# Fused attention and two MoE layers: order of SyncE's register reads, the late slot tables, and the queue of the row stores

## The chip, the cores and the metric

The kernel runs on one core of a Trainium2 chip. The metric is the device time of one execution in microseconds (us). TensorE (PE) does the matrix products, VectorE (DVE) and ScalarE (ACT) move and split what leaves PSUM, GpSimd (POOL) does some of the splitting and all gathers, and SyncE (SP) issues almost all other transfers. Each engine runs its own instructions in order.

## The reference, cut to what matters

```python
x = _attn_ref(q, k, v, beta)            # delta rule over 768 steps, 32 heads of 48
x = x.transpose(0, 2, 1, 3).reshape(3072, 384)
h = (x @ w1) * (x @ w2) @ w3            # MoE 1: one expert, width 1024
x = h @ w_out
logits = x @ w_gate + modality_bias[modality_id]      # MoE 2: top-1 of 8 experts
e_idx = np.argmax(logits, axis=1)
for e in range(8):
    mask = e_idx == e
    h = np.maximum(x[mask] @ w1[e], 0.0)
    out[mask] = gate_w[mask, None] * (h @ w2[e])
```

gate_w is the softmax probability of the chosen expert.

## The kernel before

**MoE 1.** The 3072 tokens are 12 tiles of 256. moe1 works through a tile in 8 eighths f. Each eighth does the pAB products, a chain ACT (a), DVE (a times the second product), ACT (ch), DVE (cl), and two eighths later (LAG) the px products. Attention for the next tile runs between them. When the last px of tile i is done, in eighth 1 of tile i+1, moe1_end copies the 384 columns to xr, route computes the expert and the weight on DVE, and POOL stores the two halves of xr as rows of the DRAM tensor x2. In eighths 3, 5 and 6 of tile i+1, place computes each token's place in its expert's list: small products pr, DVE steps for pos, the one-hot matrices hot (in the buffer that held xr, so they wait until the row store has read it), and the product pl, which is added to the list.

**MoE 2.** The list of tokens is cut into 14 slots, each one expert's: 3 early ones, whose table (tie) is computed in tile 10 from what the tiles before have counted, 9 full ones of 256 tokens (table tif) and 2 half ones of 128 (table tih). front reads a slot's expert and list position from its table into SyncE's registers (regs, two reads), loads the ids (id), and gathers the rows (xg, POOL). sources and load read the expert's weights in 7 pieces (r, 5 buffers, at most 4 ahead); the steps of weights split each piece into a high part (ACT) and a low part (DVE, for three of the six w1 pieces POOL, named w1l). back works through a slot in 8 eighths: ph products, ACT (hh), DVE (hl), and two eighths later the second products (spy or px). In each eighth it also takes one or two steps of the next slots' weights, in eighths 1 to 3 one step of the next slot's tokens, and one step (two in slot 1) of the generator late. late first waits three steps, then does place for tile 11, the list of ids, the full table and the half table. Slot i fetches slot i+2 in eighth 1, slot 1 in eighth 4.

**Order.** The wrapper class Engine gives each engine's instructions the order in which the program writes them. The two reads in regs go through values_load, which the wrapper does not see, so the scheduler places them on SyncE's queue as it likes. For the early slots all six reads stand ahead of the first weight reads, though the program writes the weight reads of slot 0 behind the first pair:

```python
cur["e"] = self.regs(self.early[0])
self.mid = self.middle(0, cur["e"], cur)
next(self.mid)
```

Of the kernel before, what the change touches and what calls it, by code (L numbers as in the profile page):

```python
# [21 lines left out]
P = 128  # L22
# [13 lines left out]
MT = 256  # L36
# [27 lines left out]
LAG = 2  # L64
# [39 lines left out]
class Kernel:  # L104
# [598 lines left out]
    def moe1(self, i):  # L703
        nc, m1, m2, pm = self.nc, self.m1, self.m2, self.pm
        xl, xh = (self.x[i][:, x] for x in range(2))
        passes = ((0, xh), (0, xl), (1, xh))
        for f in range(FC):
            self.slot(i + LEAD, f)
            self.at(i + LEAD, f / FC)
            g, fg = divmod(f, DCH // P)  # L710
            fs = slice(fg * P, (fg + 1) * P)
            pab = pm.tile([P, 2, MT], F32, tag="AB", name="pAB", bufs=2)
            for m in range(2):
                n = 0
                for kk in range(KC):
                    for wi, xx in passes:
                        nc.tensor.matmul(pab[:, m], self.w12[m][wi][g][kk][:, fs], xx[:, kk], start=(n == 0), stop=(n == 3 * KC - 1))
                        n += 1
            a = m2.tile([P, MT], F32, tag="a", name="a", bufs=1)
            nc.scalar.copy(a, pab[:, 0])  # L720
            nc.vector.tensor_tensor(out=a, in0=a, in1=pab[:, 1], op=ALU.mult)
            ch = m2.tile([P, MT], F32R, tag="ch", name="ch", bufs=LAG + 1)
            cl = m2.tile([P, MT], F32R, tag="cl", name="cl", bufs=LAG + 1)
            nc.scalar.copy(ch, a)
            steps = (PLAN1 if i == 0 else PLAN[(i + LEAD) % US])[f]
            if steps:
                next(self.work, None)
                self.at(i + LEAD, f / FC)
            nc.vector.tensor_tensor(out=cl, in0=a, in1=ch.bitcast(F32), op=ALU.subtract)
            self.todo.append((i, f, ch, cl))  # L730
            if len(self.todo) > LAG:
                self.second()
            if f in (5, 6) and i > 0:
                next(self.placing, None)
            if f == LAG + 1 and i > 0:
                self.placing = self.place(i - 1)
                next(self.placing)
            if f == 0 and (i + LEAD) % US == 0:
                next(self.work, None)
            if f == 6 and i + 1 < NT // MT:  # L740
                self.parts_x(i + 1)
            for _ in range(REST[f] if i == 0 and f < len(REST) else 0):
                next(self.rest, None)
            if i == 0 and f == len(REST):
                list(self.rest)
            for _ in range(steps - 1):
                next(self.work, None)
            self.at(i + LEAD, f / FC)
            if f == LAG + 1 and i == NT // MT - EB:
                self.sorting = self.early_slots()  # L750
            if i == NT // MT - EB and LAG < f <= 5:
                list(self.sorting) if f == 5 else next(self.sorting)
            if f == 5 and i == NT // MT - EB:
                self.between()
            if f == 6 and i == NT // MT - EB:
                self.listing = self.listed()
                next(self.listing)
            if f == 7 and i == NT // MT - EB:
                self.fronts()
            for _ in range(MID[(i + EB - NT // MT) * FC + f] if i >= NT // MT - EB else 0):  # L760
                next(self.mid, None)
# [12 lines left out]
    def moe1_end(self, i):  # L774
        nc, m1, m2 = self.nc, self.m1, self.m2
        self.xr = xr = m1.tile([P, TPU, DM + 1], F32, tag="xr", name="xr")
        lg = m2.tile([P, TPU, E], F32, tag="lg", name="lg")
        for t in range(TPU):
            nc.scalar.copy(xr[:, t, 0:DM], self.px[t][:, 0:DM])
            nc.vector.tensor_tensor(out=lg[:, t], in0=self.px[t][:, DM:XW], in1=self.bsel[:, i * TPU + t], op=ALU.add)  # L780
        self.route(i, lg, xr)
        for t in range(TPU):
            r = i * MT + t * P
            x = nc.gpsimd.dma_start(out=self.x2[r:r + P], in_=xr[:, t])
            for g in self.gathers:
                self.tc.declare_no_dep(x.ins, g.ins, reason="rows apart")

# [205 lines left out]
    def late_slots(self):  # L993

        nc, s1 = self.nc, self.s1
        E1 = E + 1
        one = lambda tag: s1.tile([1, E1], F32, tag=tag, name=tag)
        nf, nh, fh = one("nf"), one("nh"), one("fh")
        for t in (nf, nh):
            nc.vector.memset(t, 0.0)  # L1000
        self.count("f", self.first, -P, nf)
        yield
        full, self.nfull, _ = yield from self.table("f", MFULL - NEARLY, nf, self.first, SLOT)
        yield
        self.count("h", self.first, 0, nh)
        nc.vector.tensor_tensor(out=nh, in0=nh, in1=nf, op=ALU.subtract)
        nc.vector.scalar_tensor_tensor(out=fh, in0=nf, scalar=float(SLOT), in1=self.first, op0=ALU.mult, op1=ALU.add)
        yield
        half, self.nhalf, _ = yield from self.table("h", MHALF, nh, fh, P)
        self.full, self.half = iter(full), iter(half)  # L1010

        self.more = s1.tile([1, 1], I32, tag="more", name="more")
        nc.vector.scalar_tensor_tensor(out=self.more, in0=self.nhalf, scalar=float(NFULL - NEARLY - NHALF), in1=self.nfull, op0=ALU.add, op1=ALU.max)


    def moe2(self, early, cur):
# [2 lines left out]
        todo, states = list(early), {0: cur}  # L1019

        def late():
            for _ in range(3):
                yield
            yield from self.place(NT // MT - 1)
            yield
            yield from self.listed()
            yield
            yield from self.late_slots()

        self.late = late()  # L1030

        def fetch(i):
            if len(todo) == i < len(kinds):
                list(self.late)
                k = kinds[i]
                todo.append(self.front(next(self.full if k == "f" else self.half), k == "h"))
                self.sources(todo[i][0])

# [51 lines left out]

    def regs(self, entry):

        nc, SP = self.nc, [mybir.EngineType.SP]
        e = nc.values_load(entry[0], engines=SP, min_val=0, max_val=E - 1)
        return [e, nc.values_load(entry[1], engines=SP, min_val=0, max_val=E * NCOL)]

    def front(self, entry, small=False, r=None):

# [86 lines left out]
    def back(self, i, mi, ahead):  # L1185
# [11 lines left out]
        for f in range(FC):  # L1197
# [10 lines left out]
            nc.scalar.activation(hh, ph, AF.Relu)  # L1208
            nc.vector.scalar_tensor_tensor(out=hl, in0=ph, scalar=0.0, in1=hh.bitcast(F32), op0=ALU.max, op1=ALU.subtract)
            ahead(f in (1, 2, 3), 1 + (f < 3 if i == 0 else f > 4))  # L1210
            for _ in range(1 + (i == 1)):
                next(self.late, None)
            if f == (4 if i == 1 else 1):
                self.fetch()
            prev.append((f, hh, hl))
# [101 lines left out]
```

## Time and profile before

| | us |
|---|---|
| median of 3 runs | 867.23 (865.93 to 867.48) |
| profiled execution, its own time | 865.13 |
| its span | 863.4 |
| TensorE busy in the span | 801.3 (93%) |
| VectorE busy | 612.6 (71%) |
| ScalarE busy | 408.2 (47%) |
| GpSimd busy | 173.7 (20%) |

The span is what the trace holds of the execution; its own time lies 1.7 us above it. Products overlap, so a busy TensorE is not one at its peak: the length of a slot tells more than the busy share.

### The profile page before, as it was taken

Reading aid. Unit: us, or ns where it says so; the run is one execution under the profiler, and the core shown is the slowest. Engines: PE = TensorE matmul, PEld = TensorE weight load, DVE = VectorE, ACT = ScalarE, POOL = GpSimd, SP = SyncE. Lnnn points to the kernel's source line nnn. Section 1 sums busy time; section 2 is a strip of 40 time slices with the busy share of each in tenths; the row PEclk is TensorE's granted clock in tenths of the full one; section 3 lists DMA queues with packets and bytes.
Section 4 is the critical chain, followed back from the end, with each engine's and each line's share of the span. In section 5 each row is a group of like instructions: output and inputs, shape, how many; then the busy total and the mean of one; then the engine's idle time right before and its main releaser. Section 6 shows DMA issues by size and latency. Waiting matters only on the chain.

```text
span 863.4 us, 24832 instructions
## 1 busy us (share of the span) xinstructions
PE 801.3 (93%) x10223; PEld 742.9 (86%) x10223; DVE 612.6 (71%) x1512; ACT 408.2 (47%) x863; POOL 173.7 (20%) x196
## 2 busy tenths in 40 slices
PE   3977778999999999999999999999999999999993
PEld 3844648989999999999999999998888999999982
DVE  3997399969866987698669864457787576677641
ACT  6524964461446234614461453334544565555540
POOL 5000301010101010101010100004244564645330
PEclk8588989989999999999999999999999999999997
DMA  9834343302220213041212211037447678667610
GB/s 316 278 116 166 117 129 100 82 22 80 70 81 21 82 69 82 21 129 37 66 37 65 64 38 39 20 104 246 150 133 242 227 228 272 226 218 250 214 41 4
DMA packets 47018, 105.43 MB, mean 122 GB/s; under 512 B 9412, under 2 KB 25940, under 8 KB 46896
## 3 DMA queue, kind: packets, MB, share of 16 engines
q1 hardware_dynamic: 41424, 88.35, 32.1%
q0 software_dynamic: 5472, 15.40, 5.2%
q8 instruction: 82, 1.34, 0.6%
q14 instruction: 40, 0.33, 0.1%
HBM read 89.15 MB, written 10.63 MB: 116 GB/s over the span
## 4 chain that ended last, share of the span: by engine, by line
PE 59%; DVE 9%; issue 9%; POOL 5%; DMA 3%; ACT 1%; SPq 1%; POOLq 0%; ACTq 0%; DVEq 0%
PE pAB L84 21%; PE px L84 13%; PE ph L84 6%; PE spy L84 3%; PE py L84 2%; PE pq L84 2%; PE pu L84 2%; PE pk L84 2%; POOL w1l L84 2%; PE pS L84 2%; POOL xg L84 1%; PE pg L84 1%; PE pe L84 1%; PE pf L84 1%; DMA id<-ids 1%
## 5 line engine op out<-in xcount | busy, mean ns | idle before, releaser
L84 PE MATMUL pAB<-x,w 128*128 128x256 f32 x1728 | 233.2, 290 | 0.0
L84 PEld LDWEIGHTS pAB<-x,w 128*128 128x128 f32 x1728 | 216.4, 193 | 4.1
L84 ACT CAST ch<-a 128x256 fp32r<-128x256 f32 x96 | 38.9, 406 | 123.2 <-DVE a L84 123.2
L84 ACT COPY a<-pAB 128x256 f32<-128x256 f32 x96 | 35.6, 371 | 126.0 <-PE pAB L84 111.1
L84 POOL DMA_DIRECT2D x2d<-xr x24 | 13.5, 566 | 389.2 <-ACT TT L84 188.6
L84 DVE TENSOR_TENSOR a<-a,pAB 128x256 f32<-128x256 f32 x96 | 39.9, 416 | 73.1 <-ACT a L84 72.9
L84 PE MATMUL ph<-sxh,w1h 128*128 128x256 f32 x288 | 83.0, 288 | 2.1 <-DVE hl L84 2.1
L84 PE MATMUL ph<-sxh,w1l 128*128 128x256 f32 x288 | 81.5, 283 | 0.0
L84 PE MATMUL ph<-sxl,w1h 128*128 128x256 f32 x288 | 81.5, 283 | 0.0
L84 ACT ACTIVATE hh<-ph 128x256 fp32r<-128x256 f32 x96 | 36.9, 384 | 90.8 <-PE ph L84 90.4
L84 DVE TENSOR_TENSOR w2l<-r,w2h 128x768 fp32r<-128x768 f32 x56 | 61.6, 1113 | 12.6 <-ACT w2h L84 12.6
L84 DVE SCALAR_TENSOR_TENSOR hl<-ph,hh 128x256 fp32r<-128x256 f32 x96 | 40.3, 420 | 41.9 <-ACT hh L84 41.2
L84 DVE TENSOR_TENSOR Tt<-tmp,Tt 128x31 f32<-128x31 f32 (+15 forms) x186 | 65.0, 349 | 6.6 <-DVE tmp L84 0.2
L84 DVE TENSOR_TENSOR tmp<-Ab,Tt 128x31 f32<-128x31 f32 (+15 forms) x186 | 66.9, 360 | 3.2
L84 PE MATMUL px<-w34h,ch 128*128 128x392 f32 x192 | 66.0, 344 | 2.7 <-DVE w34l L84 1.7
L84 PE MATMUL px<-w34h,cl 128*128 128x392 f32 x192 | 65.3, 340 | 0.0
L84 PE MATMUL px<-w34l,ch 128*128 128x392 f32 x192 | 65.3, 340 | 0.0
L84 POOL TENSOR_TENSOR w1l<-r,w1h 128x512 fp32r<-128x512 f32 x39 | 50.2, 1306 | 52.6 <-ACT w1h L84 46.9
L84 PEld LDWEIGHTS ph<-sxh,w1h 128*128 128x128 f32 x288 | 55.0, 191 | 3.5 <-DVE hl L84 3.5
L84 PE MATMUL pw<-wosW,TT 128*128 128x392 f32 x80 | 38.1, 622 | 19.7 <-DVE TT L84 19.4
L84 PEld LDWEIGHTS ph<-sxh,w1l 128*128 128x128 f32 x288 | 55.1, 191 | 0.0
L84 PEld LDWEIGHTS ph<-sxl,w1h 128*128 128x128 f32 x288 | 55.0, 191 | 0.0
(262 smaller groups left out, 1736.3 us busy)
## 6 DMA issues: line engine op xcount, KB each, us to landing
r<-in_e_w_dram SPq DMA_DIRECT2D x42, 512.0 KB, 4.4
r<-in_e_w_dram SPq DMA_DIRECT2D x56, 384.0 KB, 4.7
raw<-in_w_dram SPq DMA_DIRECT2D x25, 512.0 KB, 5.4
kT<-in_kt_dram SPq DMA_DIRECT2D x12, 512.0 KB, 4.5
W<-in_q_dram SPq DMA_DIRECT2D x24, 256.0 KB, 4.2
x2d<-xr POOLq DMA_DIRECT2D x24, 192.5 KB, 2.9
vt<-in_v_dram SPq DMA_DIRECT2D x12, 384.0 KB, 4.2
kb<-in_kb_dram SPq DMA_DIRECT2D x12, 384.0 KB, 3.3
```

The source lines that it names most:

```text
L84: x = f(*a, **kw)
```

## The change

There are four parts. SyncE's register reads take the place in SyncE's order at which the program writes them. The half slots' table leaves late and becomes a generator of its own, later, with one step per eighth from the sixth slot (i = 5) on. late waits one step instead of three at its start and gets one step per eighth in slots 0 to 2, also in slot 1. The row stores of MoE 1 are issued by ScalarE in eighth 2 of the next tile, behind its ch; those of tile 11 stay with GpSimd.

```diff
@@ moe1, eighth f of tile i, behind second()
+            if f == LAG and i > 0:
+                self.put_rows(nc.scalar)
@@ moe1_end
         self.route(i, lg, xr)
+        self.rows = i, xr
+        if i == NT // MT - 1:
+            self.put_rows(nc.gpsimd)
+
+    def put_rows(self, queue):
+
+        i, xr = self.rows
         for t in range(TPU):
             r = i * MT + t * P
-            x = nc.gpsimd.dma_start(out=self.x2[r:r + P], in_=xr[:, t])
+            x = queue.dma_start(out=self.x2[r:r + P], in_=xr[:, t])
@@ late_slots
         full, self.nfull, _ = yield from self.table("f", MFULL - NEARLY, nf, self.first, SLOT)
-        yield
+        self.full, self.nf, self.nh, self.fh = iter(full), nf, nh, fh
+
+    def half_slots(self):
+
+        nc, s1, nf, nh, fh = self.nc, self.s1, self.nf, self.nh, self.fh
         self.count("h", self.first, 0, nh)
...
@@ moe2
         def late():
-            for _ in range(3):
-                yield
+            yield
             yield from self.place(NT // MT - 1)
...
-        self.late = late()
+        self.late, self.later = late(), self.half_slots()
...
-                list(self.late)
                 k = kinds[i]
+                list(self.later if k == "h" else self.late)
@@ regs
-        e = nc.values_load(entry[0], engines=SP, min_val=0, max_val=E - 1)
-        return [e, nc.values_load(entry[1], engines=SP, min_val=0, max_val=E * NCOL)]
+        for x, top in zip(entry, (E - 1, E * NCOL)):
+            loads, values = nc.values_load_multi_w_load_instructions(x, engines=[mybir.EngineType.SP], min_val=0, max_val=top)
+            if self.fixed:
+                for a in loads:
+                    if nc.sync.last is not None:
+                        self.order(a, nc.sync.last)
+                    nc.sync.last = a
+            got += values
+        return got
@@ back
-            for _ in range(1 + (i == 1)):
+            if i < NEARLY:
                 next(self.late, None)
+            elif i > NEARLY + 1:
+                next(self.later, None)
```

## Rows read from the trace of the kernel before

**Rows 1.** Windows, MoE 1: length; busy PE, PEld, DVE, ACT, POOL; clock; DMA.

```profile
180.00:560.00 380.00, 379.25 (x6406) 359.23 (x6405) 280.74 (x788) 161.42 (x343) 28.72 (x37) 1.00 0.19 58
```

**Rows 2.** Windows, slots 0 to 4, same columns.

```profile
606.60:627.30 20.70, 18.55 (x136) 18.04 (x135) 16.10 (x48) 10.96 (x25) 5.54 (x6) 1.00 0.56 172
627.30:648.20 20.90, 19.30 (x129) 17.55 (x128) 19.06 (x65) 10.37 (x22) 8.67 (x8) 1.00 0.44 130
648.20:668.45 20.25, 18.33 (x127) 17.46 (x126) 13.88 (x22) 10.37 (x22) 9.50 (x8) 0.99 0.70 235
668.45:687.40 18.95, 18.95 (x128) 18.95 (x128) 11.72 (x22) 10.49 (x22) 9.73 (x9) 0.92 0.64 218
687.40:705.00 17.60, 17.60 (x129) 17.60 (x128) 12.07 (x21) 10.37 (x22) 10.09 (x10) 1.00 0.79 261
```

**Rows 3.** Waits in 560 to 610 us: total, times, longest.

```profile
PE px L84 <- DVE lg L84: 1.0, 1, 1.0
...
PE pl L84 <- DVE hot L84: 0.8, 2, 0.6
```

**Rows 4.** Timeline of ScalarE, tiles 10 and 11: start, length, idle before and releaser.

```profile
579.74 0.62 ACT L84 CAST w1h<-r 128x512 fp32r<-128x512 f32 x1 [3.87 <-DMA r<-in_e_w_dram]
...
588.77 0.41 ACT L84 CAST ch<-a 128x256 fp32r<-128x256 f32 x1 [1.17 <-DVE a L84]
```

**Rows 5.** Timeline of SyncE's queue, tile 11.

```profile
576.16 2.04 SPq L84 DMA_DIRECT2D r<-in_e_w_dram  x4
578.39 1.87 SPq L84 DMA_DIRECT2D id<-ids  x3
```

**Rows 6.** Register reads of the tables: duration ns min/median/max, first and last start.

```profile
L1095 SPq TENSOR_LOAD <-tie x3: 263/271/280, 572.8 to 575.1; - x3
...
L1094 SPq TENSOR_LOAD <-tif x9: 262/269/316, 637.0 to 652.3; - x9
```

**Rows 7.** Chain that ended last, tile 11: start, length.

```profile
592.67 6.81 DMA x2d<-xr
```

**Rows 8.** Timeline of VectorE, tile 11.

```profile
599.58 0.31 DVE L84 TENSOR_SCALAR hot<-cols,lo,tok 128x128 f16<-128x128 bf16 x1 [1.14 <-DMA x2d<-xr]
```

**Rows 9.** Timeline of ScalarE, eighths 2 and 3 of a tile.

```profile
233.89 0.41 ACT L84 CAST ch<-a 128x256 fp32r<-128x256 f32 x1 [0.49 <-DVE a L84]
236.20 0.37 ACT L84 COPY a<-pAB 128x256 f32<-128x256 f32 x1 [1.90 <-PE pAB L84]
```

**Rows 10.** Timeline of TensorE, slot 0.

```profile
619.43 0.64 PE L84 MATMUL pl<-hot 128*128 128x192 f16 x2 [1.45 <-DVE hot L84]
```

**Rows 11.** Timeline of GpSimd, slots 0 to 4.

```profile
611.12 4.33 POOL L84 TENSOR_TENSOR w1l<-r,w1h 128x512 fp32r<-128x512 f32 x3
...
637.87 1.28 POOL L84 TENSOR_TENSOR w1l<-r,w1h 128x512 fp32r<-128x512 f32 x1 [1.51 <-ACT w1h L84]
...
656.28 1.05 POOL L84 DMA_INDIRECT xg<-x2d,id  x1 [2.53 <-DMA id<-ids]
...
659.31 2.54 POOL L84 TENSOR_TENSOR w1l<-r,w1h 128x512 fp32r<-128x512 f32 x2
...
702.88 2.54 POOL L84 TENSOR_TENSOR w1l<-r,w1h 128x512 fp32r<-128x512 f32 x2 [6.44 <-ACT w1h L84]
```

**Rows 12.** Timeline of VectorE, slot 1: two instructions of the half table and its last.

```profile
638.40 0.82 DVE L84 TENSOR_TENSOR geh<-sl 1x64 f32<-1x64 f32 x1
639.26 0.21 DVE L84 TENSOR_TENSOR geh<-geh,nh 1x64 f32<-1x64 f32 x1
...
642.53 0.15 DVE L84 SCALAR_TENSOR_TENSOR more<-tih,tif 1x1 int32<-1x1 int32 x1
```

**Rows 13.** Timeline of SyncE's queue, slot 2.

```profile
651.13 0.51 SPq L84 DMA_DIRECT2D id<-ids  x1
...
661.88 2.14 SPq L84 DMA_DIRECT2D r<-in_e_w_dram  x4
```

**Rows 14.** Timeline of ScalarE, slot 2.

```profile
665.70 0.62 ACT L84 CAST w1h<-r 128x512 fp32r<-128x512 f32 x1 [4.07 <-DMA r<-in_e_w_dram]
```

More of the change, by code (lines that the diff above doesn't have):

```diff
@@ L1009, in late_slots @@
         half, self.nhalf, _ = yield from self.table("h", MHALF, nh, fh, P)
-        self.full, self.half = iter(full), iter(half)
+        self.half = iter(half)
         self.more = s1.tile([1, 1], I32, tag="more", name="more")
@@ L1091, in regs @@
     def regs(self, entry):
-        nc, SP = self.nc, [mybir.EngineType.SP]
-        e = nc.values_load(entry[0], engines=SP, min_val=0, max_val=E - 1)
-        return [e, nc.values_load(entry[1], engines=SP, min_val=0, max_val=E * NCOL)]
+        nc, got = self.nc, []
+        for x, top in zip(entry, (E - 1, E * NCOL)):
[7 more added lines that the diff above has]
+        return got
     def front(self, entry, small=False, r=None):
```

## Prediction

> **What bounds it now.** I read the stretches first, then the waits and the engines' timelines of the stretches that are too long. The reader sees three regions. In MoE 1 with attention TensorE is busy 379.25 of 380 us at full clock [rows 1]: nothing is to be won there, only lost. A slot of MoE 2 takes 17.6 us when nothing disturbs it, as slot 4, where TensorE is busy all the time [rows 2]. Slots 0 to 3 take 20.7, 20.9, 20.25 and 18.95 us [rows 2], 80.8 in all instead of 70.4: 10.4 us are lost between the end of MoE 1 and slot 4. And tile 11, just before, holds two waits of TensorE: 1.0 us of px for DVE's lg and 0.8 us of pl for hot [rows 3], which itself waits 1.14 us for the row store of tile 10 [rows 8]. All four parts of the change work in these places, so the whole stake is about 12 us.
>
> **Register reads of the early slots.** ScalarE's first split of slot 0's weights waits 3.87 us for its read and starts at 579.74 [rows 4]. ScalarE runs in order, so the a and xr copies of tile 11 come late, DVE's lg after them, and px waits its 1.0 us. The read was issued at 576.16 [rows 5], behind six register reads; the second read of the first pair begins at 572.8 and takes 0.27 us, that of the third at 575.1 [rows 6]. So a pair takes (575.1 − 572.8)/2 = 1.15 us. In written order the four weight reads follow the first pair, at about 573.4, some 2.7 us earlier; the split then waits about 1.2 us. Bounds: 0 (something else on ScalarE is as late) to 1.0 us gained; I take 0.9, since 2.7 is more than the delay that px shows. The ids behind them go from 578.39 on now [rows 5]; the first will go about 1 us earlier, the third about 1 us later, and no product waits for them.
>
> **Row stores by ScalarE.** On GpSimd the store of tile 10 stands among gathers that wait for ids; its packets start at 592.67 and land 6.81 us later [rows 7]. ScalarE's place for it is behind ch of eighth 2, which ends at 589.18 [rows 4], or earlier with the reads above. Even with 1.2 us to issue and the same 6.81 us it lands by 597.2, and hot, which was ready for it at 599.58 − 1.14 = 598.44 [rows 8], waits for nothing: 0.8 us gained (bounds 0 to 0.8). The Trainium skill, "DMA: Bandwidth & Descriptors", section "Issuing engines are not separate DMA queues", says that the queues share the same engines and that another queue saves only issue time; by it the landing stays as long, which the sum above already allows. What ScalarE pays: no row shows it issuing a transfer. The nearest is SyncE's, three ids in 1.87 us [rows 5], so two in about 1.2. In a tile of MoE 1 ScalarE ends ch at 234.3 and idles 1.90 us before the next a [rows 9], and 1.2 fits. The stores' inputs are ready, since DVE wrote them before the a of the same eighth. So 0; if the cover were gone it would cost up to 11 × 1.2 = 13 us.
>
> **Late lists, slot 0.** place now begins in eighth 1, not 3, and the count and the first part of the full table come into slot 0. Before, pl waited 1.45 us for hot [rows 10], because DVE had pos, a weight split and hot in a row. Two eighths earlier DVE has the same row of work, but GpSimd splits w1 from 611.12 for 4.33 us [rows 11]. That matters: of two like instructions of the half table, one took 0.82 us and one 0.21 [rows 12], and the long one began inside the w1l split of GpSimd that ran from 637.87 to 639.15 [rows 11]. The Trainium skill, "SBUF — State Buffer", section "Who interferes with whom", calls this an exclusive lock: a DVE instruction with two SBUF inputs, or one in a two-port mode, waits out a GpSimd instruction that reads SBUF. The trace agrees (0.82 against 0.21 us); by that rule alone the second of the cases that follow would hold. From the rows: pl was ready at 619.43 − 1.45 = 617.98 [rows 10] and would be two eighths, 4.4 us, earlier, at 613.6. With no lock the same DVE work stands before it and the wait stays about 1.45. If the splits are waited out, four hot instructions of about 0.31 us [rows 8] from 615.45 end at 616.7, a wait of 3.1 us, 1.65 more. And if DVE gets there early the wait could go: 1.45 gained. I take a loss of 0.4, nearer the unlocked case because a split of GpSimd blocks only until its own end, one of three here.
>
> **Late lists, slot 1.** DVE is busy 19.06 of 20.9 us there against 12.07 of 17.6 in slot 4 [rows 2]. The half table's 22 instructions, about 0.21 us each [rows 12], are 4.6 us; the count and first part of the full table, some 10 instructions at the same price, are 2.1 us more, and the bunching by two per eighth go too. That leaves DVE at about 12.4 of 17.6 us, so TensorE should set the pace: at most 20.9 − 17.6 = 3.3 us gained, at least 1.5 if a wait of another kind stays. I take 2.8.
>
> **Slot 2 and its clock.** ScalarE waits 4.07 us for a weight read, until 665.70 [rows 14]. That read was issued at 661.88 [rows 13], when GpSimd's two w1l from 659.31 for 2.54 us [rows 11] had freed its buffer. These stand behind the gathers, the first of which waited 2.53 us for ids [rows 11] that SyncE issued at 651.13 [rows 13]. SyncE was late because the scheduler put the reads of all full slots, two times 9, between 637.0 and 652.9 [rows 6], in front of weight reads and ids. Now each slot has its pair, 1.15 us, right before its ids. The 18 reads at half a pair each, 0.57 us, are 10 us of the 16 in that stretch, so without them SyncE is ready earlier, less the pair's 1.15 us: I take the ids 1 us earlier, and the gathers, which waited 2.53 us, with them; chain 1.0 to 2.3 us earlier. The product wait at the end of the slot is 2.65 us (20.25 − 17.6); I take 1.8 gained, bounds −1.15 (the pair only adds) to 2.65. After that wait the granted clock of slot 3 averages 0.92, full clock for most of it and the level of 1.2 GHz for a part [rows 2], which is 18.95 − 17.6 = 1.35 us. pl's wait of 1.45 us left slot 0 at 1.00 [rows 2, 10], so with under 1 us of wait I expect full clock: 1.0 gained, bounds −1.0 (the clock falls for longer) to 1.35.
>
> **Later slots.** Each pair stands 1.15 us before its ids. GpSimd idles 6.44 us before its next split in slot 4 [rows 11], so a later gather is covered; I take 0.2 lost for slot 3, where the slack is least. The half table's 4.6 us of DVE now fall into eighths 0 to 4 of slot 5, where DVE should be as free as in slot 4, busy 12.07 of 17.6 us [rows 2]. An eighth lasts 2.2 us, hl has about one to spare (ph has two buffers), and the table adds about 1 us in each of five eighths while some 0.6 us per eighth are free: 0.1 lost, bounds 0 to 1.6 (half of what both tables cost in slot 1).
>
> **The sum.** 0.9 + 0.8 − 0.4 + 2.8 + 1.8 + 1.0 − 0.2 − 0.1 = 6.6 us. The profiled execution took 865.13 us, its span 863.4 and 1.7 around it; it would take 858.5. It lies 2.1 us under the median of the runs, 867.23, and I apply the same gain there: 860.6.
>
> **Rivals.** (1) Slot 2's wait stays: the pair before the ids takes back what the freed queue gives, the gathers stay late, the clock falls again. For it: the chain through GpSimd is the same, and buffers, not SyncE, release the last read. Against: the ids' own issue is early by 1 us. Gain 6.6 − 1.8 − 1.0 = 3.8: 863.4. (2) Slot 0 grows by the waited-out splits (1.25 more than taken), and slot 1 gains only 1.5: 6.6 − 1.25 − 1.3 = 4.05, 863.2; with (1) as well 1.25, no change that can be measured: 866.0. (3) Slower: the pair before each slot's ids, written after weight reads that wait for buffers, makes the gathers of every slot late, and GpSimd's w1 splits and the next weight reads with them. Its place is slots 2 to 11; the price is up to 1.15 us in each, 11.5, less the 6.6 elsewhere without slot 2 and 3 (3.8): 867.2 + 7.7 = 874.9. It decides if ids land later than the 6.44 us of GpSimd's slack [rows 11] can take, which 1.15 us does not reach. (4) The change's reads do not move anything, since weight reads wait for buffers anyway: only slots 0, 1 and the row store count, 0.8 − 0.4 + 2.8 − 0.1 = 3.1: 864.1.
>
> **Chances and range.** The forecast as summed, 857 to 862.5: 0.55. Rivals (1), (4) or (2) alone, 862.5 to 865.4: 0.30. No change that can be measured (within 0.2%, 1.7 us, about what a measurement of this kernel can tell): 0.09. Slower: 0.06, mostly (3). So faster 0.85. The range runs from 856.9 (a gain of 10.3: the upper bounds 1.0, 0.8, 3.3, 2.65 and 1.35 and 1.2 of slot 0's 1.45) to 865.6, which leaves out the last two cases and a little below.
>
> **What would show it.** In the changed profile: the first w1h split of slot 0 starts near 577; no wait of hot for x2d; slot 1 near 18 us with DVE busy about 13; slot 2 under 19 with ids issued about 2 us into it; slot 3 at clock 1.00; slot 5 still 17.6. I am wrong if pl's wait in slot 0 passes 3 us, if ScalarE's wait for the weight read in slot 2 is still 4 us, or if any tile of MoE 1 shows TensorE waiting for a.

## The result and the profile after

The changed kernel takes 859.07 us (median of 4 runs, 855.77 to 860.27) beside 867.36 us (865.93 to 870.02) for the kernel before on the same chip: a ratio of 0.9895, 95% interval 0.9858 to 0.9931, 8.3 us faster. Run again later it took 857.6 us beside 865.72. The profiled execution took 855.77 us with a span of 854.0, 9.4 us less than before.

Where the 9.4 us lie follows from TensorE's timeline. The table cuts both spans at the first product pr, at the pr that stands in tile 11, and then at the first ph product of each slot (lengths in us; "changed, again" is the second run of the same kernel).

| stretch | before | changed | gain | changed, again |
|---|---|---|---|---|
| start to the first pr | 197.93 | 195.97 | 1.96 | 197.98 |
| MoE 1 up to the pr in tile 11 | 391.57 | 390.33 | 1.24 | 390.32 |
| from there to slot 0 | 17.17 | 16.23 | 0.94 | 16.50 |
| slot 0 | 20.59 | 22.17 | −1.58 | 22.16 |
| slot 1 | 20.74 | 17.71 | 3.03 | 17.72 |
| slot 2 | 20.25 | 19.75 | 0.50 | 19.38 |
| slot 3 | 19.00 | 17.49 | 1.51 | 17.48 |
| slot 4 | 17.62 | 17.63 | 0 | 17.63 |
| slot 5 | 17.64 | 18.19 | −0.55 | 18.19 |
| slots 6 and 7 | 35.12 | 35.12 | 0 | 35.12 |
| slot 8 to the end | 105.80 | 103.38 | 2.42 | 103.41 |

The first line is not the change's: over all the profiles below the start lies between 196.0 and 198.6 us, with old and new order alike (one kernel that changes the start itself left aside). So 7.5 us of the 9.4 are to be explained.

The windows of MoE 1 and of slots 0 to 5 in the changed kernel answer to [rows 1, 2]; the columns are the same, and the ends lie up to 0.2 us from the cuts of the table.

```profile
180.00:560.00 380.00, 379.11 (x6461) 359.06 (x6461) 280.57 (x797) 161.45 (x343) 16.70 (x17) 1.00 0.20 58
...
602.50:624.86 22.36, 18.75 (x137) 18.14 (x136) 19.15 (x59) 11.15 (x25) 5.50 (x6) 1.00 0.56 160
624.86:642.20 17.34, 17.34 (x125) 17.20 (x125) 14.67 (x33) 10.38 (x22) 10.10 (x8) 1.00 0.48 149
642.20:662.33 20.13, 18.43 (x131) 18.06 (x130) 12.50 (x22) 10.68 (x22) 8.58 (x8) 1.00 0.74 247
662.33:679.81 17.48, 17.48 (x128) 17.48 (x128) 12.34 (x21) 10.50 (x22) 9.68 (x9) 1.00 0.71 222
...
697.44:715.63 18.19, 18.19 (x128) 17.49 (x128) 15.89 (x43) 10.29 (x22) 10.24 (x10) 1.00 0.73 222
```

MoE 1 is as full as before: ScalarE's stores cost TensorE nothing. Slot 1 is full now, with DVE at 14.67 us instead of 19.06 [rows 2]. Slot 0 has grown, with DVE busy 19.15 us instead of 16.10. Slot 2 still has 1.7 us in which TensorE isn't busy, but the clock stays at 1.00 in slot 3, which was 0.92.

The waits of the changed kernel from slot 0 to slot 4 (total, times, longest) name two new ones of spt, the products that turn the gathered rows xg; sxl is the low part of rows turned before.

```profile
PE pl L84 <- DVE hot L84: 1.9, 1, 1.9
...
PE spt L84 <- DMA xg<-x2d,id: 1.7, 2, 1.4
...
PE spt L84 <- DVE sxl L84: 1.1, 1, 1.1
```

ScalarE's timeline answers to [rows 4, 9, 14]. The first split of slot 0's weights waits 1.78 us instead of 3.87. The two row stores are issued by ScalarE's queue (ACTq) in 0.81 us beside its ch. In tile 11 there is no gap for them: the next split, which came right behind ch before, comes 0.45 us behind it. The 4.07 us of slot 2 have become 0.26 and 0.86.

```profile
575.70 0.62 ACT L84 CAST w1h<-r 128x512 fp32r<-128x512 f32 x1 [1.78 <-DMA r<-in_e_w_dram]
...
585.16 0.81 ACTq L84 DMA_DIRECT2D x2d<-xr  x2
586.01 0.62 ACT L84 CAST w1h<-r 128x512 fp32r<-128x512 f32 x1 [0.45 <-ACT ch L84]
...
658.43 0.62 ACT L84 CAST w1h<-r 128x512 fp32r<-128x512 f32 x1 [0.26 <-DMA r<-in_e_w_dram]
...
660.94 0.62 ACT L84 CAST w1h<-r 128x512 fp32r<-128x512 f32 x1 [0.86 <-DMA r<-in_e_w_dram]
```

SyncE's queue, answering to [rows 5, 13]: in tile 11 the weight reads go at 571.96 instead of 576.16, and in slot 2 the ids 1.1 us after the slot's first product (642.41), which was 3.1 us before.

```profile
571.96 2.05 SPq L84 DMA_DIRECT2D r<-in_e_w_dram  x4
...
643.54 0.50 SPq L84 DMA_DIRECT2D id<-ids  x1
```

DVE's timeline in slots 0 and 5 shows where those grew. Its small steps of 2 to 16 elements take 0.16 us when nothing is beside them, like lo below (hi and lo are the column and the row of a token's place). Three of place's took 0.64, 1.00 and 1.24 us, and one of the half table's 1.57. The last hot step of place ends at 613.02, 10.5 us into slot 0.

```profile
608.19 0.64 DVE L84 TENSOR_TENSOR pos<-pos,oh 128x16 f32<-128x16 f32 x1
608.87 0.17 DVE L84 TENSOR_REDUCE pf<-pos 128x2 f32<-128x16 f32 x1
609.08 1.00 DVE L84 TENSOR_SCALAR hi<-pf 128x2 f32<-128x2 f32 x1
610.11 1.24 DVE L84 TENSOR_SCALAR hi<-hi 128x2 f32<-128x2 f32 x1
611.38 0.16 DVE L84 SCALAR_TENSOR_TENSOR lo<-hi,pf 128x2 f32<-128x2 f32 x1
...
612.75 0.27 DVE L84 TENSOR_SCALAR hot<-cols,hi 128x192 f16<-128x192 bf16 x1
...
700.09 1.57 DVE L84 TENSOR_TENSOR nh<-nh,nf 1x9 f32<-1x9 f32 x1
```

GpSimd's timeline has a split of w1 at each of these times (the step of 700.09 begins 0.24 us ahead of its split), and lo begins when the splits of slot 0 have ended (606.98 + 4.30 = 611.28). The two gathers in between are slot 3's.

```profile
606.98 4.30 POOL L84 TENSOR_TENSOR w1l<-r,w1h 128x512 fp32r<-128x512 f32 x3
...
637.39 1.73 POOL L84 DMA_INDIRECT xg<-x2d,id  x1 [1.45 <-DMA id<-ids]
639.42 1.77 POOL L84 DMA_INDIRECT xg<-x2d,id  x1 [0.31 <-issue]
...
700.33 1.30 POOL L84 TENSOR_TENSOR w1l<-r,w1h 128x512 fp32r<-128x512 f32 x1
```

The chain that ended last runs through the second of them in the changed kernel, and TensorE's spt of slot 2 begins 0.04 us after its 7.25 us.

```profile
639.42 7.25 DMA xg<-x2d,id
```

And the end, which no row ahead of the prediction shows. These are two instructions of GpSimd behind the last output store, from the view of one line's instructions (duration ns min/median/max, first and last start), first before, then changed:

```profile
L1312 POOLq DRAIN  x3: 46/99/7418, 854.8 to 863.1; - x3
...
L1080 POOLq INC_SWDGE_SEM  x1: 1996/1996/1996, 852.8 to 852.8; - x1
```

```profile
L1333 POOLq DRAIN  x3: 46/99/5622, 847.5 to 853.7; - x3
...
L1092 POOLq INC_SWDGE_SEM  x1: 1560/1560/1560, 845.9 to 845.9; - x1
```

Together they are 7182 ns instead of 9414, 2.23 of the 2.42 us that the stretch from slot 8 on became shorter.

### The profile page after: what moved, and what is told of

It is laid out like the page before. It is cut to its first block, busy times and chain, and to the rows that moved or that the text cites. A ratio compares the mean times of both kernels' runs of the same rounds, so it can differ in the third digit from the quotient of the medians.

```text
span 854.0 us, 24817 instructions
## 1 busy us (share of the span) xinstructions
PE 796.9 (93%) x10223; PEld 739.6 (87%) x10223; DVE 613.7 (72%) x1512; ACT 409.6 (48%) x863; POOL 162.7 (19%) x174
## 4 chain that ended last, share of the span: by engine, by line
PE 62%; DVE 8%; issue 8%; POOL 4%; ACT 1%; DMA 1%; SPq 0%; POOLq 0%; ACTq 0%; DVEq 0%
PE pAB L84 23%; PE px L84 14%; PE ph L84 7%; PE spy L84 4%; PE py L84 2%; PE pq L84 2%; PE pk L84 2%; PE pu L84 2%; PE pS L84 2%; POOL w1l L84 2%; PE pg L84 1%; PE pe L84 1%; DVE Tt L84 1%; POOL out_dram L84 1%; DVE tmp L84 1%
## 5 line engine op out<-in xcount | busy, mean ns | idle before, releaser
L84 DVE TENSOR_TENSOR w2l<-r,w2h 128x768 fp32r<-128x768 f32 x56 | 59.3, 1071 | 12.3 <-ACT w2h L84 12.1
L84 POOL TENSOR_TENSOR vt<-vt,rb 128x768 f32<-128x768 f32 x12 | 18.2, 1519 | 201.6 <-DMA vt<-in_v_dram 117.7
L84 DVE TENSOR_TENSOR cl<-a,ch 128x256 fp32r<-128x256 f32 x96 | 40.4, 421 | 19.6 <-ACT ch L84 18.8
## 6 DMA issues: line engine op xcount, KB each, us to landing
x2d<-xr ACTq DMA_DIRECT2D x22, 192.5 KB, 3.0
```

What stands on the lines that cost most here:

```text
L84: x = f(*a, **kw)
```

## The experiments

The ratios are to the kernel before on the same chip, in brackets the 95% interval. "Span less start" is the profiled span without the part up to the first pr; it is 665.5 us before, 658.0 and 657.9 in the two profiles of the changed kernel. The first four runs took the change apart.

**Row stores alone.** The kernel before, with put_rows and its call in eighth 2 only.

```diff
+            if f == LAG and i > 0:
+                self.put_rows(nc.scalar)
```

> The kernel before with one part of the change: the row stores of tiles 0 to 10 by ScalarE. My theory: it only frees hot in tile 11 from its 1.14 us wait for the store, so the stretch from tile 11's pr products to slot 0's first ph (17.2 us before, 16.2 us after the whole change) becomes 16.2 to 16.5 us, MoE 1 keeps its length (391.5 us from the first pr to tile 11's), and the time falls by about 0.8 us, too little to measure. Rival, stores cost ScalarE time on the path: the 391.5 us grow by 1 us per tile or part of it. Second rival: GpSimd's queue matters more than the wait shows, and the gain is 2 us or more.

863.35 us, ratio 0.9961 [0.9946, 0.9976]. From the pr in tile 11 to slot 0 it takes 17.36 us, so the store alone gives nothing there. hot no longer waits for the store, but VectorE comes to it 10.26 us behind pr, where before it was ready at 8.94. Of these 1.3 us, 0.65 are a wait for ScalarE's split, ahead of which the two issues stand; the rest is in two small steps (eq 0.35 and sm 0.70 us instead of 0.17). ScalarE, then VectorE, of this run:

```profile
591.16 0.62 ACT L84 CAST w1h<-r 128x512 fp32r<-128x512 f32 x1 [0.45 <-ACT ch L84]
```

```profile
591.81 0.69 DVE L84 TENSOR_TENSOR w1l<-r,w1h 128x512 fp32r<-128x512 f32 x1 [0.65 <-ACT w1h L84]
```

The end gives most of the gain: 103.42 us from slot 8 on instead of 105.80. (Its profile had a read wait of 6.3 us in slot 2, where the order before has 4.07.)

**Register reads alone.** The kernel before, with the new regs only.

```diff
-        e = nc.values_load(entry[0], engines=SP, min_val=0, max_val=E - 1)
...
+                    self.order(a, nc.sync.last)
```

> The kernel before with one part of the change: the register reads in written order. My theory: the first weight split of slot 0 waits 1.8 us instead of 3.9, px in tile 11 no longer waits for lg (1.0 us gained), and in slot 2 the wait for the weight read (4.07 us) and the dip of the clock in slot 3 go, together 2 to 4 us; slot 1 stays near 20.9 us because VectorE sets it. Time 3 to 5 us lower. Rival: slot 2's wait hangs on GpSimd's gathers, not on SyncE, and stays within 0.5 us; then only about 1 us is gained. Second rival: the pair before each slot's ids makes slots 2 and later longer than before.

859.87 us, ratio 0.9931 [0.9909, 0.9954]: half of the whole gain. MoE 1 goes to 390.32 us, slot 2 to 17.64 and slot 3 to 18.04; slot 1 stays at 20.74 and the end at 106.0. So the written order by itself takes away the late first reads and TensorE's wait in slot 2; ScalarE still waits there for reads, 1.23 and 1.36 us instead of 4.07.

**Half table alone.** The kernel before with half_slots and later; late keeps its three waits, and slot 1 its two steps per eighth.

```diff
-        self.late = late()
+        self.late, self.later = late(), self.half_slots()
...
+            if i > NEARLY + 1:
+                next(self.later, None)
```

> The kernel before with one part of the change: the half slots' table leaves late and runs from the sixth slot on; late keeps its three waiting steps and its two steps per eighth in slot 1. My theory: slot 1 falls from 20.9 to 18 to 19 us, because 4.6 us of VectorE's work go, and slot 5 grows by 0.6 us as it did with the whole change (18.19 for 17.5); slot 2's wait for its weight read stays. Time 1.5 to 2.5 us lower. Rival: slot 1 needs all three parts (one step per eighth too) and stays above 20 us. Second rival: with slot 1 shorter, slot 2's wait grows by as much and nothing is gained.

863.66 us, ratio 0.9971 [0.9955, 0.9987]. Slot 1 takes 18.95 us: of the 3.0 us that slot 1 gives, the half table is 1.8 and the fourth part, one step per eighth and place moved ahead, the other 1.2. Slot 5 takes 18.16, the loss of the changed kernel. The read wait of slot 2 did not stay as expected: ScalarE waits 1.97 us, slot 2 takes 18.78 and slot 3 17.84. With 4.07 us before and 6.3 with the stores alone, the wait differs by more than 2 us among the three profiles in which the scheduler places the reads, so what a single pair of profiles says of slot 2 is uncertain by that. (This profile also has 19.79 us from tile 11 to slot 0, where pl waits 1.77 us for hot, and 19.18 us in slot 4, where ph waits 1.28 us for hl.)

**The change with late as it was.** The changed kernel, but place of tile 11 again in eighth 3 of slot 0, and two steps per eighth in slot 1.

```diff
-            yield
+            for _ in range(3):
+                yield
...
-            if i < NEARLY:
+            for _ in range(1 + (i == 1)):
                 next(self.late, None)
```

> The changed kernel with one part undone: late waits three steps at its start again and takes two steps per eighth in slot 1, so place of tile 11 begins in eighth 3 of slot 0. My theory: in the changed kernel slot 0 takes 22.36 us against 20.7 before, because VectorE's small steps for pos and hi (0.64, 1.00 and 1.24 us, against 0.17) are held up while GpSimd splits w1; begun in eighth 3 they meet no split, and slot 0 falls back to about 20.7, 1.6 us gained; slot 1 gets 2 us of table work back but has room and stays under 18.3. Time 1 us lower than the changed kernel, 858 us or a little under. Rival: slot 1 grows by as much as slot 0 gains, as VectorE was its limit before, and the time stays or rises.

854.62 us (854.35 to 856.65), ratio 0.9873 [0.9856, 0.9891]: faster than the changed kernel, whose second run has 0.9918 [0.9899, 0.9937]; the interval of the first, 0.9858 to 0.9931, takes it in. Slots 0 to 3 take 20.64, 18.95, 18.27 and 17.47 us; span less start is 656.5, 1.5 us less. The three parts multiplied, 0.9961 × 0.9931 × 0.9971 = 0.9864, agree with it. So the fourth part, moving place ahead and spreading its steps, wins 1.2 us in slot 1 and loses more in slots 0 and 2.

The next runs ask why, and what the end has to do with the stores.

**Half of the stores back on GpSimd.**

```diff
-            x = queue.dma_start(out=self.x2[r:r + P], in_=xr[:, t])
+            x = (queue if t else self.nc.gpsimd).dma_start(out=self.x2[r:r + P], in_=xr[:, t])
```

> The changed kernel, with the first of each tile's two row stores (11 of 22) back on GpSimd in the same place. Theory: the end of the program, where GpSimd's closing drain took 7418 ns with 22 more stores and 5622 ns with none of them, grows with the number of GpSimd's stores: 11 of them give a drain of about 6520 ns and a closing semaphore step of about 1780 ns, and the stretch from slot 7's first ph to the span's end about 104.6 us (105.8 before, 103.4 changed). Time about 1.2 us above the changed kernel's on this chip. Rival: the end differs for another cause (who stored last, or chance), then 103.4 or 105.8 and nothing between.

(The stretch meant is that from the first ph of slot 8, the ninth slot.) 859.02 us, ratio 0.993 [0.9914, 0.9946], beside 857.6 for the changed kernel on the same chip. From slot 8 on 104.52 us, and the two instructions, in the same view as above:

```profile
L1333 POOLq DRAIN  x3: 46/99/6520, 847.8 to 854.8; - x3
...
L1092 POOLq INC_SWDGE_SEM  x1: 1780/1780/1780, 845.9 to 845.9; - x1
```

(7418 − 6520) / 11 = 82 ns and (1996 − 1780) / 11 = 20 ns for each store, the same as between none and all. The end grows with GpSimd's transfers.

**The changed kernel again.**

```diff
 (no edit)
```

> The changed kernel once more, beside the others of this chip. Theory: 857 to 859 us, slot 0 about 22.2, slot 1 17.7, slot 2 about 19.7 with TensorE's spt waiting for slot 3's gather, slot 5 18.2. Rival: the losses in slots 0 and 2 belong to that one profile; then these slots come out at 20.6 and 17.7 here.

857.6 us (856.77 to 860.77), ratio 0.9918 [0.9899, 0.9937]; slots as in the table above. The losses in slots 0, 2 and 5 are the kernel's, not the profile's.

**Half table only in eighths 2 to 4**, on top of the run with late as it was.

```diff
-            if i > NEARLY + 1:
+            if i > NEARLY + 1 and 2 <= f <= 4:
```

> The kernel of the fourth run (changed, with late's three waits and two steps per eighth in slot 1), and the half table's steps only in eighths 2 to 4 of the slots from the sixth on. Theory: the 0.55 us that slot 5 lost come from small DVE steps of the half table that wait beside GpSimd's w1l split in eighths 0 and 1; without them slot 5 takes 17.6 to 17.7 us, 0.5 us less than the fourth run. Rival: the table's DVE work itself fills the eighths; then the loss of about 0.5 moves to eighths 2 to 4 and to slot 6.

855.52 us, ratio 0.9877 [0.9859, 0.9896]. Slot 5 takes 17.64 us and slot 6 17.49, as the theory said; in the time it can't be seen, since slots 2 and 3 were 1.1 us longer in this profile than in the run that it builds on.

**One step per eighth, place as before.** The run with late as it was, but a single step in slot 1 too.

```diff
-            for _ in range(1 + (i == 1)):
-                next(self.late, None)
+            next(self.late, None)
```

> The kernel of the fourth run with one step of late per eighth in slot 1 as well, so that the bunching goes while place of tile 11 stays where it was before. Theory: slot 1 goes from 18.95 to about 17.7 us with slot 0 still at 20.6: 1.2 us less than the fourth run. Rival: the full table is then ready only in eighth 4 of slot 1, slot 3's ids and gather come late, and spt waits in slot 2 as in the changed kernel (about 1.5 to 2 us), so that nothing or a loss of up to 1 us is left.

860.61 us, ratio 0.9939 [0.9922, 0.9956]: the rival, and more than it said. Slot 1 takes 18.11 us, but the full table is ready only 12.1 us into it, and slot 2 takes 24.21, with a granted clock of 0.86. TensorE's timeline there:

```profile
649.82 1.07 PE L84 MATMUL spt<-ident,xg 128*128 128x128 f32 x2 [3.86 <-DMA xg<-x2d,id]
```

The wait goes with the gathers' lead. Taken from the start of slot 3's second gather to the first product of slot 2, it is 5.8 us before and with the reads alone, and there is no wait; 3.9 us in the run with late as it was and in the one built on it, where spt waits 0 and 0.85 us for the gather; 3.0 in the changed kernel, 1.39; −0.6 here, 3.86. But the lead is not all: at the same 3.0 us the wait is 1.21 us in the second profile of the changed kernel and 1.74 in the run with half of the stores. The other part is how long the gathers are on their way. These are the issues around slot 3's two gathers, with the median us to landing, first before (640.5 to 643.3 us), then changed (637.2 to 641.3):

```profile
xg<-x2d,id POOLq DMA_INDIRECT x2, 3.3
```

```profile
r<-in_e_w_dram SPq DMA_DIRECT2D x2, 512.0 KB, 5.8
r<-in_e_w_dram SPq DMA_DIRECT2D x2, 384.0 KB, 7.0
xg<-x2d,id POOLq DMA_INDIRECT x2, 7.4
```

Before, no weight read is issued beside them; in the changed kernel four are. With the reads alone there is none either, and they take 3.3 us; with late as it was there are three, and they take 6.0. The products need the rows 2.9 us into slot 2. The lead, 2.8 us shorter, would by itself have landed the second gather about 0.3 us into the slot, and the longer way by itself 1.4 us into it: only the two together make the wait. No run moved the reads alone, so that they are what holds the gathers up is argued.

**GpSimd fills instead of splitting, slot 1's weights.** The changed kernel; the three pieces are set to zero, so the low part of half of slot 1's w1 is left out.

```diff
+                if i == 1 and kk * W1N + n >= W1D:
+                    nc.gpsimd.memset(w1l[:, kk, gs].bitcast(F32), 0.0)
+                else:
...
```

> The changed kernel, in which GpSimd, instead of computing its three pieces of the low part of slot 1's w1 (during slot 0), fills them with zeros, which reads no SBUF (a part of slot 1's product is left out so). Theory: slot 0 lost 1.6 us because place's small DVE steps wait for GpSimd's splits; with the fills pos<-pos,oh and the two hi steps take about 0.17 us again instead of 0.64 to 1.24, spt's wait of 1.15 us for sxl and pl's of 1.85 us for hot shrink, and slot 0 takes about 20.6 us instead of 22.2. Rival: the bunching of DVE's own work in eighths 1 to 3 is the cause; then the steps are short but the waits and 22.2 us stay. Second rival: a fill holds DVE up as a split does; then the steps stay long for a shorter time, slot 0 about 21.5.

854.71 us, ratio 0.9871 [0.9847, 0.9894]. DVE's timeline, the same steps as above (GpSimd's three fills run from 609.14 to 610.63):

```profile
610.48 0.17 DVE L84 TENSOR_TENSOR pos<-pos,oh 128x16 f32<-128x16 f32 x1
...
610.88 0.17 DVE L84 TENSOR_SCALAR hi<-pf 128x2 f32<-128x2 f32 x1
611.09 0.17 DVE L84 TENSOR_SCALAR hi<-hi 128x2 f32<-128x2 f32 x1
...
612.66 0.26 DVE L84 TENSOR_SCALAR hot<-cols,hi 128x192 f16<-128x192 bf16 x1
```

pos<-pos,oh is short beside a fill, and the two hi steps are short because the fills, 1.49 us in a row instead of 4.30, have just ended. The last hot step ends 8.1 us into slot 0 instead of 10.5, and pl's wait is gone; spt's wait for sxl stays at 1.14 us. Slot 0 takes 21.39 us, 0.8 less than in the changed kernel, but this is not the whole effect: its granted clock is 0.92 in this profile, where both profiles of the changed kernel have 1.00. The run with half of the stores on GpSimd, whose slot 0 is the changed kernel's, has 0.92 there too. Slot 0 as a window, with the columns of [rows 1], and pl on TensorE's timeline, of that run and then of this one:

```profile
602.69:624.86 22.17, 20.13 (x135) 19.51 (x134) 19.06 (x59) 11.02 (x25) 5.49 (x6) 0.92 0.56 161
...
612.81 0.64 PE L84 MATMUL pl<-hot 128*128 128x192 f16 x2 [0.30 <-DVE hot L84]
```

```profile
604.83:626.22 21.39, 19.79 (x135) 19.47 (x135) 16.80 (x59) 11.12 (x25) 2.67 (x6) 0.92 0.57 166
...
614.48 0.33 PE L84 MATMUL pl<-hot 128*128 128x192 f16 x2
```

With half of the stores TensorE came to pl 9.82 us into the slot instead of 8.29 in the changed kernel, pl waited 0.30 us instead of 1.85, and the slot took the same 22.17 us. So in the changed kernel it is hot that sets the length of slot 0, and what delays TensorE ahead of pl, spt's wait too, costs nothing there. With the fills TensorE came to pl 9.65 us into the slot, 1.36 us later than in the changed kernel, and found hot ready. Without that the slot would take about 20.0 us, an estimate from these rows (21.39 − 1.36). So the splits cost about 2.1 us, more than the 1.6 that slot 0 lost. The theory holds for pl and for the slot, the rival for spt's wait alone.

**Full table early.** The changed kernel with late's three waits, two steps in eighths 5 to 7 of slot 0 and in eighth 0 of slot 1, slot 3 fetched in eighth 2, and the half table in eighths 2 to 4.

```diff
-            if i < NEARLY:
+            for _ in range(1 + (i == 0 and f > 4 or i == 1 and f == 0)):
                 next(self.late, None)
...
-            if f == (4 if i == 1 else 1):
+            if f == (2 if i == 1 else 1):
```

> The changed kernel with late's three waits again (place of tile 11 clear of GpSimd's splits), two steps of late in eighths 5 to 7 of slot 0 and in eighth 0 of slot 1, slot 3 fetched in eighth 2 of slot 1, and the half table's steps only in eighths 2 to 4. Theory: slot 2's spt wait comes from slot 3's gather, which starts too late because the full table is ready 8.6 us into slot 1, when slot 1 itself is 3 us shorter; with the table ready about 5 us into slot 1 the gather lands in time. Slots 0 to 3 then take about 20.6, 17.8, 17.7 and 17.5 us, slot 5 17.6: 4.5 to 5 us less than the changed kernel, about 853. Rivals: the three double eighths fill DVE at the end of slot 0, which then takes 21.5 to 22 us (gain 3 to 4); or the gather still waits behind the weight reads on the DMA engines, since these start earlier too, and 1 to 2 us of spt's wait stay in slot 2.

856.04 us, ratio 0.9881 [0.9861, 0.9901], not the 853 expected. spt's wait is gone: the second gather starts 8.6 us ahead of slot 2. But ScalarE's read wait is back, and with it 20.39 us of slot 2 and a clock of 0.92 in slot 3. ScalarE, then GpSimd, of this run:

```profile
662.52 0.62 ACT L84 CAST w1h<-r 128x512 fp32r<-128x512 f32 x1 [4.06 <-DMA r<-in_e_w_dram]
```

```profile
636.21 1.03 POOL L84 DMA_INDIRECT xg<-x2d,id  x1 [0.31 <-issue]
637.27 2.56 POOL L84 TENSOR_TENSOR w1l<-r,w1h 128x512 fp32r<-128x512 f32 x2
```

With the fetch two eighths earlier the gathers stand ahead of two of GpSimd's three splits, and these now end at 639.83, 13.9 us into slot 1, where the changed kernel's end at 635.26, 10.6 us into it. The r buffers come free later, and the reads come later with them. Neither theory nor rivals had that; the last run below, with the fetch back in eighth 4, bears it out, since TensorE no longer waits there for a read.

**Six transfers of the start off GpSimd**, on top of the run before.

```diff
-            nc.gpsimd.dma_start(out=self.x2[NT - (t + 1) * P:NT - t * P], in_=zero)
+            nc.scalar.dma_start(out=self.x2[NT - (t + 1) * P:NT - t * P], in_=zero)
...
```

> The kernel of the run before, and six more transfers off GpSimd: the four stores of zero rows and two small loads at the program's start are issued by ScalarE. Theory: the closing drain and semaphore step shorten by 82 and 20 ns for each, 5622 to about 5130 ns and 1560 to about 1440 ns, 0.6 us at the end. Rival: the end counts only transfers that were still to be reclaimed late in the program, not those of the start; then 5622 and 1560 stay. At the start ScalarE's An copies come up to 2.4 us (six issues of 0.4 us) later, which TensorE may or may not feel.

858.86 us, ratio 0.9912 [0.989, 0.9934]. The end shortens by the rule, (5622 − 5132) / 6 = 82 ns and (1560 − 1440) / 6 = 20 ns each, so transfers of the start count as well. But the start grows to 202.4 us, 4 more than in the run before, and that costs more than the 0.6 us are worth.

```profile
L1334 POOLq DRAIN  x3: 46/103/5132, 852.7 to 858.4; - x3
...
L1093 POOLq INC_SWDGE_SEM  x1: 1440/1440/1440, 851.2 to 851.2; - x1
```

**All of it with the gathers in place.** The changed kernel with late's three waits, an eighth between hot and pl, the steps dealt anew, the fetch in eighth 4 as in the changed kernel, and the half table in eighths 2 to 4.

```diff
+        if i == NT // MT - 1:
+            yield
         pl = self.ps.tile([P, E * NCOL], F32, tag="ps", name="pl")
...
+            for _ in range({(0, 6): 2, (0, 7): 3, (1, 1): 2}.get((i, f), 1)):
```

> The changed kernel with late's three waits, one eighth more between hot and pl of tile 11, two steps of late in eighth 6 and three in eighth 7 of slot 0, two in eighth 1 of slot 1, slot 3 fetched in eighth 4 of slot 1 as in the changed kernel, and the half table's steps only in eighths 2 to 4. Theory: with slot 3's gathers again behind GpSimd's third w1l split, the splits, the buffers and the weight reads come as early as in the changed kernel, so that ScalarE's read wait of 4 us in slot 2 goes; with the full table ready 2 us earlier the gathers wait for no ids, and spt's wait goes too; pl comes an eighth after hot and its 1.45 us go. Slots 0 to 3: about 19.3, 17.8, 17.7 and 17.5 us, slot 5 17.6; 7 us less than the changed kernel, about 851. Rival: the gather's time on the way is set by the weight reads on the same DMA engines and 1 us or more of spt's wait stays; or the five steps in two eighths fill DVE at the end of slot 0 and give back what pl gains; then 853 to 855.

854.68 us (853.47 to 855.52), ratio 0.9865 [0.9835, 0.9895]; span less start 655.5, the shortest of all. Slot 0 takes 18.70 us, since pl waits for nothing; slots 2 and 3 take 18.17 and 17.88, with 0.32 us of spt's wait. But slot 1 takes 20.17: two steps of the full table fell beside GpSimd's splits (628.60 and 630.99, 1.28 and 1.27 us long), and ph waited 1.48 us for the hl behind them. DVE's timeline:

```profile
628.63 1.37 DVE L84 TENSOR_TENSOR ohf<-eff,sl 1x108 f32<-1x108 f32 x1
...
631.07 1.22 DVE L84 CAST tif<-tabf 1x25 int32<-1x25 f32 x1
```

This, the run with late as it was and the one with the half table in eighths 2 to 4 beat the kernel before, at 854.6 to 855.5 us. Their intervals don't tell them apart; they lie below that of the changed kernel's second run, but not below that of its first.

## Why the prediction was right, and where its terms were off

The predicted time, 860.6 us, lies 1.5 us above the median, within the range. The gain came out near the sum because one term that was missing made up for three that were too kind: without start and end the stretches gained 5.1 us where the sum said 6.6, and the end gave 2.4 more. The direction and the main terms were reasoned; that the total fits so closely is luck. Two of the signs that it named did not come: slot 2 takes 19.75 us instead of under 19, and slot 5 18.19 instead of 17.6.

**Register reads of the early slots: right.** 0.9 was said, MoE 1 gained 1.24. The first split starts at 575.70; with the start 1.96 us earlier that is 577.7 on the clock of [rows 4], where 577 was said, and its wait is 1.78 us instead of the 1.2 worked out. The run with the reads alone gives all of it (390.32 us), and so rules out rival (4).

**Row stores: right in place and size** (0.8 said, 0.94 found), with one correction: ScalarE's price of 0 holds for MoE 1, 390.33 us beside 390.32 with the reads alone, but not in tile 11. ScalarE pays 0.81 us for two, less than the 1.2 taken from SyncE; in tile 11 its next split and VectorE's behind it come later by that, which is why the stores alone gave nothing there. With the reads in order, VectorE is early enough: hot starts 9.1 to 9.4 us behind pr in the two profiles, and pl waits at most 0.16 us. The Trainium skill, "DMA: Bandwidth & Descriptors", section "Issuing engines are not separate DMA queues", agrees so far: from issue to landing the page of the profile has 3.0 us in the median on ScalarE's queue, 2.9 on GpSimd's. In tile 11 the earlier issue was enough: with the 6.81 us of [rows 7] the store of 585.16 would still have landed by 592.8, ahead of hot at 595.44.

**Slot 0: of its two cases the prediction took the wrong one.** The step that failed is "I take a loss of 0.4, nearer the unlocked case because a split of GpSimd blocks only until its own end, one of three here". It lost 1.58. The splits came in an unbroken row, and place's steps fell right into it, one behind the other: pos<-pos,oh waited 0.5 us more and the two hi steps 0.8 and 1.1, each until a split ended (608.83, 610.08 and 611.35; the splits end at 608.80, 610.05 and 611.28). The other case, the splits waited out, was close: it has hot done at 616.7, 10.0 us into slot 0, where the trace has 10.5, and a loss of 1.65. That pl waited 1.85 us and not the 3.1 of that case comes from TensorE being late itself, by spt's wait of 1.15 us for sxl, which was in no step; as the run with half of the stores shows, this wait costs nothing while hot is later still. The Trainium skill's rule in "SBUF — State Buffer", section "Who interferes with whom", fits what ran and what didn't: pos<-pos,oh with two SBUF inputs waited, the reduction pf with one did not, and a GpSimd fill, which reads no SBUF, left pos<-pos,oh at 0.17 us. The hi steps, with one input, waited too; the rule allows for that in a two-port mode, but no run here shows which mode a step was in. For spt's wait the kernel suggests a cause: pr now stands between two spt in TensorE's order, and both use the same two PSUM buffers (ps); in the run where pr comes two eighths later spt doesn't wait. No run took the buffers apart, so this is argued, not shown.

**Slot 1: right.** 2.8 was said, 3.03 found. DVE at 14.67 us rather than 13 made no difference, as TensorE sets the pace. Of it 1.8 is the half table and 1.2 the fourth part; the single step without the earlier place gives 0.8 of that (18.11 us instead of 18.95).

**Slot 2: the wait named went, another took its place.** The passage "the gathers, which waited 2.53 us, with them" holds for slot 4's gathers and the reads behind them: ScalarE's wait fell from 4.07 us to 0.26 and 0.86. But the term was 1.8 and slot 2 gained 0.5 (0.87 in the second profile; the read wait of the order before is itself uncertain by 2 us, as said at the run with the half table alone). What was left out is the gather of slot 3, which the prediction didn't price: the full table came 8.6 us into slot 1 instead of 9.5, but slot 1 ended 3 us sooner, and with weight reads issued beside it the gather was 7.4 us on its way instead of 3.3. The rows under the run with one step per eighth show both. This is rival (1) in part: a wait stayed, but by a different path, and without the clock.

**Slot 3's clock: right in kind, larger in size.** TensorE stood still for 1.39 us in slot 2, and the clock stayed at 1.00 in slot 3, so all 1.5 us came back, not 1.0. Where ScalarE's read made it wait at the slot's end, in the run with the full table early, it was 0.92 again. But the reason given, a wait of under 1 us, is not what the runs show: waits of 1.39 us here and 1.74 with half of the stores left the clock at 1.00, while behind spt's wait of 1.15 us in slot 0 it was 1.00 in two profiles and 0.92 in two others (the one with the fills counted). Whether it falls behind a wait of this length is not settled by these runs.

**Later slots.** The 0.2 us set aside for the pairs of reads were not taken: slot 4 and those behind it take 17.6 us with the reads alone and in the changed kernel. Rival (3) has no sign in any run. Slot 5 lost 0.55, not 0.1, inside the bounds, and not by the table's own DVE time but by one step of 1.57 us, most of it beside a split; with the table two eighths later it was gone.

**Missing: the end.** The prediction counted the stores' issue and landing, and gave no price to the program's close. Its 2.42 us are a quarter of the profiled gain. With it the sum would have been 9.0, above the 7.5 found.

## What to carry to other kernels

When a stage is shortened, look at what has to be ready for the next one by then, above all at gathers and tables whose time doesn't shrink with it, and may grow when other transfers move beside them. Some small VectorE steps are cheap only away from GpSimd's elementwise work: place them by GpSimd's timeline, not by VectorE's busy share. Look at a stage's granted clock, and at which wait ends last in it, before its length is taken for the effect of an edit. And count what GpSimd issues over the whole program, since its closing drain stood at the end of every run here.

## What the runs showed of the hardware that was not expected

- GpSimd's close grows with the number of transfers that it issued in the whole program: with 0, 11, 22 and 28 of them moved to ScalarE, DRAIN took 7418, 6520, 5622 and 5132 ns and INC_SWDGE_SEM 1996, 1780, 1560 and 1440, 82 and 20 ns less for each.
- A DVE step of 2 elements per partition took 1.24 us beside a GpSimd split and 0.17 alone; one of 16 elements took 0.64 beside a split and 0.17 beside a fill.
- ScalarE issues two transfers of 192.5 KB in 0.81 us beside its own work: its ch of 585.15 and the stores of 585.16 overlap in the timeline. Its next instruction came 0.45 us behind ch.
- The same order of work ran slot 0 at a granted clock of 1.00 in two profiles and of 0.92 in another, with the same 22.17 us, because TensorE's loss fell into a wait for VectorE.
